# Packed attention with routed experts: the guess's sums formed on VectorE, and the temperature carried by the embeddings

## The chip, the cores and the metric

One core of one Trainium2 chip runs the kernel. The metric is the device time of one execution in microseconds (us), as the median of several runs.

## The reference

```python
def _attn_ref(q, k, v, p):          # 8 batches, 8 heads, 576 rows, 64 wide; 32 packing queries p
    p_packed = sm_attn(p, k, v)     # softmax attention of p over k, v
    return sm_attn(q, p_packed, p_packed)

def _moe_ref(x, expert_emb, tau, w1, w2):      # x: 4608 rows of 512; 8 experts, 1024 hidden
    xn = x / (norm(x) + 1e-06)
    en = expert_emb / (norm(expert_emb) + 1e-06)
    logits = xn @ en.T / tau
    expert_idx = np.argmax(logits, axis=1)
    probs = softmax(logits)
    gate_w = probs[arange(N), expert_idx]
    out[mask] = gate_w[mask, None] * (np.maximum(x[mask] @ w1[e], 0.0) @ w2[e])   # mask: rows of expert e
```

All arrays are fp32.

## The kernel before

The kernel goes batch by batch. For one batch, attention 1 packs keys and values into 32 rows for each head; attention 2 lets the 576 queries look at these 32 rows; then one expert is applied to all 576 rows. Which expert that is, is guessed early for the whole batch, so that its weights can be loaded in time. Rows that go to another expert are counted (`counts`), and a loop at the end of the program repairs such batches; it is skipped if there are none.

**The order of the work** is the order in which generators are stepped. `ffn(b)` is the outer stream: hidden products (L1004, `hidden`), the last 64 rows' output products (L1039), and the main output products (L1057). After each of its steps one step of the next batch's attention stream `att_main(b + 1)` is emitted, so that each engine executes the two batches' instructions interleaved, in exactly the order written. For batch 0 the table `PLAN` says which stream is stepped.

**The guess.** In `att1` (`pack`) the packed rows of both head groups become pair rows (`pair_rows`, tile `ppx`), TensorE transposes them (`pair_turn`, L501), VectorE copies the result to SBUF (tile `T`, L568; L598 in `pack_slowly`, the path of batch 1). `row_logits` (L512) multiplies `T` with the expert embeddings `enT`: for each pair row its 8 logits, which `logits_out` (L521) copies behind the pair rows into `ppx`, where the route's products (L766) read them later. `guess` (L619) needs the sum of these logits over all packed rows: two products of the tile `itaus` (1/tau in all places) with the logits (L629), accumulated. Then VectorE finds the largest (L635, L636), and `sel` (L640) marks it. The index goes to a register of the engine that issues the loads of `w1` and `w2`.

**The queries' turns.** Four VectorE instructions `kt<-nat` (L291, 0.78 us each) turn the queries of a batch; `next(queries)` places them between the steps of attention 1 and of the guess. The fourth, the turn of head pair 3, is placed behind `sel`. `query_scores` (L270) then computes the scores in `rounds`: 16 products, in groups of four by head group; the seventh is the first to read the turned queries of head pair 3.

**The temperature.** `enT` holds the normalised embeddings without 1/tau. `route` multiplies its logits `lg` by `itau` (L822); the guess has 1/tau in `itaus`.

**The splitting of w2.** While the hidden products of the second half run, ScalarE casts a part of `w2` (L909) and GpSimd subtracts it from the original (L910, `w2s`), 8 times for each batch; both operands of the subtraction lie in SBUF.

Of the kernel before, what the change touches and what calls it, by code (L numbers as in the profile page):

```python
# [9 lines left out]
F32 = mybir.dt.float32  # L10
# [4 lines left out]
ALU = mybir.AluOpType  # L15
AX = mybir.AxisListType

P = 128
# [9 lines left out]
def kernel(  # L28
# [12 lines left out]
    nc = tc.nc  # L41
    B, H, S, D = q.shape
    E, DM, F = w1.shape
    NP = p.shape[2]
    NG = H // HB
    NPR = H // 2
# [70 lines left out]
    def drain(g):  # L117
        for _ in g:
            pass

    itau = cp.tile([P, 1], F32, name="itau")
    fold = cp.tile([P, 32], F32, name="fold")
    itaus = cp.tile([P, 64], F32, name="itaus")
    enT = cp.tile([P, NPR, E], F32, name="enT")

    def embeddings():

        emb_sb = sb.tile([E, DM], F32, name="emb_sb", tag="st", bufs=2)
        yield nc.scalar.dma_start(emb_sb, emb)
        seen = sm.tile([1, 1], F32, name="seen", bufs=1)  # L130
        nc.scalar.activation(seen, ones[:1], AF.Exp)
        yield
        esq = sb.tile([E, DM], F32, name="esq", tag="st", bufs=2)
        ess = sm.tile([E, 1], F32, name="ess", bufs=1)
        nc.scalar.activation(esq, emb_sb, AF.Square, accum_out=ess)
        yield
        rq = sm.tile([E, 1], I32, name="rq", bufs=1)
        nc.vector.tensor_scalar(
            out=rq, in0=ess.bitcast(I32), scalar1=-0.5, scalar2=float(0x5F3759DF),
            op0=ALU.mult, op1=ALU.add,  # L140
        )
        yield
        hx, t, ery, enrm = (
            sm.tile([E, 1], F32, name=name, bufs=1) for name in ("hx", "rt", "ery", "enrm")
        )
        nc.gpsimd.tensor_scalar_mul(hx, ess, -0.5)
        cur = rq.bitcast(F32)
        for _ in range(3):
            nc.gpsimd.tensor_scalar(
                out=t, in0=hx, scalar1=cur, scalar2=cur, op0=ALU.mult, op1=ALU.mult  # L150
            )
            nc.gpsimd.tensor_scalar(
                out=ery, in0=t, scalar1=1.5, scalar2=cur, op0=ALU.add, op1=ALU.mult
            )
            cur = ery
        nc.gpsimd.tensor_scalar(
            out=enrm, in0=ess, scalar1=ery, scalar2=1e-6, op0=ALU.mult, op1=ALU.add
        )
        yield
        nc.vector.reciprocal(enrm, enrm)  # L160
        yield
        en_sb = sb.tile([E, DM], F32, name="en_sb", tag="st", bufs=2)
        nc.gpsimd.tensor_scalar(out=en_sb, in0=emb_sb, scalar1=enrm, scalar2=None, op0=ALU.mult)
        yield
        pt = ps.tile([P, 512], F32, name="pf", tag="pf")
        for pr in range(NPR):
            nc.tensor.transpose(
                pt[:, pr * E : (pr + 1) * E], en_sb[:, pr * P : (pr + 1) * P], ident[:E, :E]
            )
        yield  # L170
        nc.scalar.copy(enT.rearrange("a b c -> a (b c)"), pt[:, : NPR * E])

    class Batch:
        def __init__(self):
# [78 lines left out]
    def idle(n):  # L253
        for _ in range(n):
            yield
# [253 lines left out]
    def row_logits(x, pt, gs=range(NG)):  # L509
        for g in gs:  # L510
            for pr in range(2):
                nc.tensor.matmul(  # L512
                    pt[64 * pr : 64 * pr + 64, g * E : (g + 1) * E],
                    x.T[:, g * P + 64 * pr : g * P + 64 * pr + 64],
                    enT[:, 2 * g + pr, :],
                    start=True,
                    stop=True,
                )

    def logits_out(x, pt):  # L520
        nc.vector.tensor_copy(x.ppx[:, :, 2 * D :], pt[:, : NG * E].rearrange("p (g e) -> p g e", g=NG))  # L521

# [5 lines left out]
    def att1(x, nat, queries=None, other=None):  # L528

        def pack(queries, other):  # L530
            pack_tiles(x)
            if not x.s1:
                quarter_banks(x)
            quarter_scores(x)
            yield
            for g in range(NG):
                quarter_max(x, g)
            yield
            yield from whole_max(x)
            yield from idle(2)  # L540
            for g in range(NG):
                for n in range(HB):
                    quarter_exp(x, g, n)
                    if n:
                        yield
                quarter_flip(x, g)
            yield
            pt = pb.tile([P, 1024], F32, name="pt", tag="pb")
            for g in range(NG):
                quarter_values(x, g, nat(2 * NPR + g), pt[:, g * D : g * D + D])  # L550
            sums = pt[:, NG * D : NG * D + NG * QW // 8]
            quarter_totals(x, sums)
            if other:
                counts(other, pt[:1, 256 : 256 + NC5 * E])
            next(queries)
            yield
            if other:
                counted(other)
            quarter_sums(x, sums.rearrange("p (g k) -> p g k", g=NG))
            for g in range(NG):  # L560
                pair_rows(x, g, pt[:, g * D : g * D + D])
            yield
            next(queries)
            yield
            pu = pc.tile([P, 512], F32, name="pu", tag="pu")
            for g in range(NG):
                pair_turn(x, g, pu)
            nc.vector.tensor_copy(x.T, pu[:, 0 : NG * P])  # L568
            yield from idle(2)
            pt = pc.tile([P, 512], F32, name="pu", tag="pu")  # L570
            row_logits(x, pt)
            yield
            logits_out(x, pt)
            next(queries)
            yield

        def pack_slowly():
            pack_tiles(x)
            for g in range(NG):
                pt = pb.tile([P, 1024], F32, name="pt", tag="pb")  # L580
                p1_turn(x, g, pt)
                yield
                p1_evac(x, g, pt)
                key_sum(x, g)
                yield
            pt = pb.tile([P, 1024], F32, name="pt", tag="pb")
            for g in range(NG):
                pack_values(x, g, nat(2 * NPR + g), pt[:, g * D : g * D + D])
            yield
            for g in range(NG):  # L590
                pair_rows(x, g, pt[:, g * D : g * D + D])
            yield
            pu = pc.tile([P, 512], F32, name="pu", tag="pu")
            yield
            for g in range(NG):
                pair_turn(x, g, pu)
            yield
            nc.vector.tensor_copy(x.T, pu[:, 0 : NG * P])  # L598
            yield
            pt = pc.tile([P, 512], F32, name="pu", tag="pu")  # L600
            row_logits(x, pt)
            logits_out(x, pt)
            yield

        if x.halves:
            for g in range(NG):
                key_max(x, g)
                yield
                key_exp(x, g)
                yield  # L610
            yield from pack_slowly()
        else:
            asked = queries or all_queries(x, nat)
            yield from pack(asked, other)
            if queries is None:
                drain(asked)


    def guess(x, late=0, engine=mybir.EngineType.Pool, total=None):  # L619
        pt = pc.tile([P, 512], F32, name="pu", tag="pu")  # L620
        if total is not None:

            for n in range(NPR):
                nc.tensor.matmul(
                    pt[:1, :E], total[:, n : n + 1], enT[:, n], start=(n == 0), stop=(n == NPR - 1)
                )
        else:
            for g in range(NG):
                nc.tensor.matmul(  # L629
                    pt[:64, :E], itaus, x.ppx[:, g, 2 * D :], start=(g == 0), stop=(g == NG - 1)  # L630
                )
        yield
        m8 = sm.tile([1, 8], F32, name="m8", tag="m8", bufs=1)
        idx = sm.tile([1, 8], U32, name="idx", tag="idx", bufs=1)
# [5 lines left out]
        nc.vector.tensor_scalar(  # L640
            out=x.sel, in0=ecol[:1], scalar1=gi, scalar2=None, op0=ALU.is_equal
        )
        yield from idle(late)
        x.e = nc.values_load(
            idx[0:1, 0:1], engines=[engine], min_val=0, max_val=E - 1,
# [111 lines left out]
    def route(x):  # L757
# [36 lines left out]
        if x is bat[0]:  # L794
            for c in range(NC5):
                pt = units()
# [22 lines left out]
            nc.vector.tensor_tensor(out=lg[64:, 4], in0=lg[64:, 4], in1=lg4[64:], op=ALU.add)  # L819
            nc.vector.tensor_tensor(out=ss[64:, 4:5], in0=ss[64:, 4:5], in1=ss4[64:], op=ALU.add)  # L820

        nc.vector.tensor_scalar_mul(lg, lg, itau)  # L822
        mx = sm.tile([P, NC5, 1], F32, name="lmx", tag="lmx")
        nc.vector.tensor_reduce(mx, lg, axis=AX.X, op=ALU.max)
        nc.vector.tensor_tensor(
# [333 lines left out]
    def begin():  # L1159
# [158 lines left out]
                start=True, stop=True,  # L1318
            )
        total = sm.tile([P, NPR], F32, name="total", tag="total", bufs=1)  # L1320
        nc.vector.tensor_scalar_mul(total, pt[:, :NPR], itau)
        both_rows(1)
        queries(0, 0, nc.scalar.copy)
        g_guess = guess(x, 0, mybir.EngineType.SP, total)
# [54 lines left out]
        for g in range(NG):  # L1379
            y.s1[g] = turn_bank()  # L1380
            parity_scores(y.s1[g], wy, kT, g, lambda c: head(g, c))
            yield
        nc.gpsimd.tensor_copy(itaus, itau.broadcast_to([P, 64]))
        nc.vector.tensor_reduce(
            fold, ident.rearrange("p (a j) -> p j a", j=32), axis=AX.X, op=ALU.add
        )
# [141 lines left out]
    with tc.If(n_rest > 0):  # L1528
        with tc.For_i(0, B, 1) as b:
            nb = nc.values_load(rest_i[0:1, ds(b, 1)], min_val=0, max_val=S)  # L1530
            with tc.If(nb > 0):
# [2 lines left out]
                nat = lambda i: load_nat(b, i)  # L1534
                drain(keys(x, nat, pn))
                drain(att1(x, nat))
                drain(att2(x))
                drain(route(x))
                counts(x)
# [78 lines left out]
```

## Time and profile before

| | |
|---|---|
| median of 3 runs | 420.41 us (420.27 to 420.61) |
| the profiled execution's own time | 420.91 us |
| its span, from first to last instruction | 419.2 us |
| mean granted TensorE clock | 0.995 |
| busy: TensorE, weight loads, VectorE, ScalarE, GpSimd | 97%, 78%, 73%, 48%, 38% |

In the profile PE is TensorE's products, PEld its weight loads, DVE VectorE, ACT ScalarE, POOL GpSimd. An fp32 product of the program stands as two passes in the trace, so x8 at L512 is four products. The shares are averages over stages of different kinds.

### The profile page before, as it was taken

Reading aid. Unit: us, or ns where it says so; the run is one execution under the profiler, and the core shown is the slowest. Engines: PE = TensorE matmul, PEld = TensorE weight load, DVE = VectorE, ACT = ScalarE, POOL = GpSimd, SP = SyncE. Lnnn points to the kernel's source line nnn. Section 1 sums busy time; section 2 is a strip of 40 time slices with the busy share of each in tenths; the row PEclk is TensorE's granted clock in tenths of the full one; section 3 lists DMA queues with packets and bytes.
Section 4 is the critical chain, followed back from the end, with each engine's and each line's share of the span. In section 5 each row is a group of like instructions: output and inputs, shape, how many; then the busy total and the mean of one; then the engine's idle time right before and its main releaser. Section 6 shows DMA issues by size and latency. Waiting matters only on the chain.

```text
span 419.2 us, 11033 instructions
## 1 busy us (share of the span) xinstructions
PE 408.4 (97%) x4036; PEld 327.9 (78%) x4037; DVE 307.2 (73%) x941; ACT 202.5 (48%) x473; POOL 158.7 (38%) x197
## 2 busy tenths in 40 slices
PE   7899999999999999999999999999999999999993
PEld 4758677697878978698777978789786987779783
DVE  3677696588977889769886889778897798566500
ACT  4577705762365714754146622656146631576110
POOL 2345714437204561336414381136613273142200
PEclk9999999999999999999999999999999999999998
DMA  8999896977999479886999669886899819310012
GB/s 225 331 338 236 220 296 221 229 189 187 298 298 235 116 216 294 284 201 172 267 316 228 169 172 280 301 216 177 225 317 262 195 39 344 121 48 5 20 48 54
DMA packets 42607, 87.93 MB, mean 210 GB/s; under 512 B 11690, under 2 KB 20906, under 8 KB 42546
## 3 DMA queue, kind: packets, MB, share of 16 engines
q1 hardware_dynamic: 35280, 61.44, 54.2%
q0 software_dynamic: 6720, 25.17, 18.4%
q8 instruction: 34, 0.56, 0.6%
q10 hardware_dynamic: 546, 0.54, 0.6%
q14 instruction: 27, 0.22, 0.2%
HBM read 77.68 MB, written 9.44 MB: 208 GB/s over the span
## 4 chain that ended last, share of the span: by engine, by line
PE 91%; DMA 4%; ACT 1%; DVE 1%; POOL 1%; SPq 0%; issue 0%; ACTq 0%; POOLq 0%
PE pf L1057 43%; PE pf L1004 24%; PE pf L1039 7%; PE pt L766 5%; DMA nat<-in_k 4%; PE pt L934 3%; PE pt L396 2%; PE pt L270 2%; PE pt L331 2%; PE pt L1233 1%; PE pu L501 0%; DMA out<-o 0%; PE pt L477 0%; PE pu L512 0%; ACT st L689 0%; PE pt L464 0%
## 5 line engine op out<-in xcount | busy, mean ns | idle before, releaser
L1057 PE MATMUL pf<-w2s,hT 128*128 128x512 f32 (+1 forms) x792 | 183.9, 388 | 0.0
L1057 PEld LDWEIGHTS pf<-w2s,hT 128*128 128x128 f32 x792 | 143.1, 188 | 39.3 <-issue 9.4
L910 POOL TENSOR_TENSOR w2s<-w2r,w2s 128x512 fp32r<-128x512 f32 x64 | 81.2, 1285 | 86.1 <-ACT w2s L909 85.3
L1004 PE MATMUL pf<-AT,G 128*128 128x288 f32 x720 | 102.1, 298 | 0.4 <-DVE hT L1009 0.2
L1004 PEld LDWEIGHTS pf<-AT,G 128*128 128x128 f32 x720 | 97.2, 188 | 4.3 <-issue 1.5
L1009 DVE SCALAR_TENSOR_TENSOR hT<-pf,hT 128x224 fp32r<-128x224 f32 (+1 forms) x128 | 52.2, 413 | 30.3 <-ACT hT L1008 29.9
L1008 ACT ACTIVATE hT<-pf 128x224 fp32r<-128x224 f32 (+1 forms) x128 | 49.3, 386 | 42.8 <-PE pf L1004 40.1
L1406 ACT ACTIVATE o<-pf,gate 128x512 f32<-128x512 f32 (+1 forms) x41 | 26.0, 635 | 32.2 <-PE pf L1057 21.2
L909 ACT CAST w2s<-w2r 128x512 fp32r<-128x512 f32 x64 | 38.7, 618 | 0.2
L291 DVE STREAM_TRANSPOSE kt<-nat 128x576 f32<-128x576 f32 x52 | 38.1, 759 | 0.0
L778 ACT ACTIVATE scr<-pt 128x512 f32<-128x512 f32 (+2 forms) x47 | 25.0, 532 | 18.0 <-PE pt L766 17.0
L1039 PE MATMUL pf<-w2r,h 128*64 128x256 f32 x256 | 33.3, 388 | 0.0
L715 POOL TENSOR_TENSOR AT<-at,AT 128x576 fp32r<-128x576 f32 x7 | 9.9, 1411 | 49.1 <-ACT AT L710 49.1
L383 POOL TENSOR_TENSOR qs<-p 128x320 f32<-128x320 f32 x12 | 10.6, 881 | 45.4 <-ACT p L364 45.4
L689 ACT ACTIVATE st<-st 128x576 f32<-128x576 f32 (+1 forms) x17 | 11.1, 657 | 33.8 <-DVE st L686 32.6
L872 ACT ACTIVATE lg<-lg 128x40 f32<-128x40 f32 x8 | 1.9, 237 | 48.4 <-DVE lg L868 48.4
L781 DVE TENSOR_REDUCE lg<-pt 128x8 f32<-128x32 f32 (+2 forms) x47 | 8.7, 185 | 22.0 <-ACT scr L778 21.7
L766 PEld LDWEIGHTS pt<-ppx,at 64*128 64x128 f32 x320 | 19.7, 186 | 6.2 <-issue 3.6
L1039 PEld LDWEIGHTS pf<-w2r,h 128*64 128x64 f32 x256 | 19.4, 137 | 4.9 <-PE pu L501 1.0
L766 PE MATMUL pt<-ppx,at 64*128 64x136 f32 x320 | 23.1, 287 | 0.0
L710 ACT CAST AT<-at 128x576 fp32r<-128x576 f32 x15 | 10.1, 675 | 22.6 <-DVE at L704 22.5
L364 ACT ACTIVATE p<-pt,qnm 128x160 f32<-128x160 f32 x48 | 17.8, 398 | 0.0
(213 smaller groups left out, 474.9 us busy)
## 6 DMA issues: line engine op xcount, KB each, us to landing
nat<-in_q SPq DMA_DIRECT2D x112, 140.0 KB, 3.5
nat<-in_k SPq DMA_DIRECT2D x96, 140.0 KB, 4.0
w1t<-in_moe_w POOLq DMA_DIRECT2D x12, 1024.0 KB, 9.3
w2r<-in_moe_w POOLq DMA_DIRECT2D x24, 512.0 KB, 16.0
out<-o SPq DMA_DIRECT2D x124, 64.0 KB, 2.1
w2r<-in_moe_w SPq DMA_DIRECT2D x8, 512.0 KB, 10.3
vn<-in_v SPq DMA_DIRECT2D x24, 160.0 KB, 3.8
vn<-in_v SPq DMA_DIRECT2D x48, 80.0 KB, 3.9
```

The costliest lines, as they stand in the source:

```text
L291: nc.vector.transpose(kt.rearrange("p (c i) -> p c i", i=32), t)
L364: nc.scalar.activation(x.p1[g][:, n * QW : n * QW + QW], area(x, g)[:, n // 2, n % 2], AF.Exp, bias=x.nm[:, at : at + 1],)
L766: nc.tensor.matmul(to[:, half], x.at[at, g, n : n + P], x.ppx[at, g], start=True, stop=True, tile_position=(64 * half, 0),)
L778: nc.scalar.activation(scr[r, :, : pt.shape[2]], pt[r, :, :, : 2 * D], AF.Square, accum_out=sss[r])
L909: nc.scalar.copy(t[:, 0], raw)
L910: nc.gpsimd.tensor_tensor(out=t[:, 1], in0=raw, in1=t[:, 0].bitcast(F32), op=ALU.subtract)
L1004: nc.tensor.matmul(pf[:, :HS], w, r, start=(n == 0), stop=(n == len(ops) - 1))
L1008: nc.scalar.activation(hT[:, 0, f, cs], pf[:, :n], AF.Relu)
L1009: nc.vector.scalar_tensor_tensor(out=hT[:, 1, f, cs], in0=pf[:, :n], scalar=0.0, in1=hT[:, 0, f, cs].bitcast(F32), op0=ALU.max, op1=ALU.su ...
L1039: nc.tensor.matmul(pf[64 * hf : 64 * hf + 64, :256], h4[:, f], x.w2r[f // 2][:, f % 2, hf * 256 : hf * 256 + 256], start=(f == 0), stop=(f ...
L1057: nc.tensor.matmul(pf[:, :w], hT[:, a, f, c * P : (c + 1) * P], x.w2s[f][:, m, at : at + w], start=(f == 0 and i == 0), stop=(f == NF - 1 ...
L1406: nc.scalar.activation(o[:, :w], pf[:, :w], AF.Copy, scale=x.gate[:, c : c + 1])
```

## The change

VectorE now forms the sums for the guess itself: `whole_rows` adds up the turned pair rows in `T` (one value for each of the four head pairs and each of 128 places), multiplies `enT` with these sums, and adds over the pairs; what is left is one column of 8 values for each of the 128 partitions, `x.part`. One product of a tile of ones (`equal`) with `x.part` adds over the partitions. It stands in `guess` right behind the row logits, which have moved there; `logits_out` follows behind `sel`. `enT` is multiplied by 1/tau when it is made, and `route` no longer multiplies.

```diff
-    itaus = cp.tile([P, 64], F32, name="itaus")
+    equal = cp.tile([P, 64], F32, name="equal")
...
-        nc.scalar.copy(enT.rearrange("a b c -> a (b c)"), pt[:, : NPR * E])
+        nc.scalar.mul(enT.rearrange("a b c -> a (b c)"), pt[:, : NPR * E], itau)
...
+    def whole_rows(x):
+
+        total = sm.tile([P, NPR], F32, name="total", tag="total", bufs=1)
+        nc.vector.tensor_reduce(
+            total, x.T.rearrange("p (n j) -> p n j", n=NPR), axis=AX.X, op=ALU.add
+        )
+        part = sm.tile([P, NPR, E], F32, name="part", tag="pbd", bufs=1)
+        nc.vector.tensor_tensor(
+            out=part, in0=enT, in1=total.unsqueeze(2).broadcast_to([P, NPR, E]), op=ALU.mult
+        )
+        x.part = sm.tile([P, E], F32, name="parts", tag="parts", bufs=1)
+        nc.vector.tensor_reduce(
+            x.part, part.rearrange("p n e -> p e n"), axis=AX.X, op=ALU.add
+        )
...
             nc.vector.tensor_copy(x.T, pu[:, 0 : NG * P])
+            whole_rows(x)
             yield from idle(2)
-            pt = pc.tile([P, 512], F32, name="pu", tag="pu")
-            row_logits(x, pt)
-            yield
-            logits_out(x, pt)
             next(queries)
-            yield
+            yield from idle(2)
...
             nc.vector.tensor_copy(x.T, pu[:, 0 : NG * P])
-            yield
-            pt = pc.tile([P, 512], F32, name="pu", tag="pu")
-            row_logits(x, pt)
-            logits_out(x, pt)
+            whole_rows(x)
             yield
...
-            for g in range(NG):
-                nc.tensor.matmul(
-                    pt[:64, :E], itaus, x.ppx[:, g, 2 * D :], start=(g == 0), stop=(g == NG - 1)
-                )
+            row_logits(x, pt[:, E:])
+            nc.tensor.matmul(pt[:64, :E], equal, x.part, start=True, stop=True)
...
+        if total is None:
+            logits_out(x, pt[:, E:])
         yield from idle(late)
...
-        nc.vector.tensor_scalar_mul(lg, lg, itau)
...
-        nc.vector.tensor_scalar_mul(total, pt[:, :NPR], itau)
+        nc.vector.tensor_copy(total, pt[:, :NPR])
...
-        nc.gpsimd.tensor_copy(itaus, itau.broadcast_to([P, 64]))
+        nc.gpsimd.memset(equal, 1.0)
```

On VectorE, from the last hidden product of one batch to the fourth turn of the next batch's queries, the kernel before has these instructions (`h` is the last 64 rows' hidden values, `kt` a turned query pair, `m`, `idx`, `gi` and `sel` the guess):

```order
L568 COPY T<-pu 128x256
L1009 SCALAR_TENSOR_TENSOR hT<-pf,hT 128x224
L1014 TENSOR_SCALAR h_1302<-pf 128x64
L521 COPY ppx<-pu 128x2x8
L291 STREAM_TRANSPOSE kt<-nat 128x576
L635 MAX m_1653<-pu 1x8
L636 MAX_INDEX idx<-m_1653,pu 1x8
L638 CAST gi<-idx 1x1
L640 TENSOR_SCALAR sel<-ecol,gi 1x8
L291 STREAM_TRANSPOSE kt<-nat 128x576
```

and the changed kernel, whose line numbers are larger by some, has these:

```order
L583 COPY T<-pu 128x256
L523 TENSOR_REDUCE total<-T 128x4
L527 TENSOR_TENSOR part<-enT,total 128x32
L531 TENSOR_REDUCE parts<-part 128x8
L1017 SCALAR_TENSOR_TENSOR hT<-pf,hT 128x224
L1022 TENSOR_SCALAR h_1304<-pf 128x64
L291 STREAM_TRANSPOSE kt<-nat 128x576
L642 MAX m_1658<-pu 1x8
L643 MAX_INDEX idx<-m_1658,pu 1x8
L645 CAST gi<-idx 1x1
L647 TENSOR_SCALAR sel<-ecol,gi 1x8
L536 COPY ppx<-pu 128x2x8
L291 STREAM_TRANSPOSE kt<-nat 128x576
```

Three instructions came in behind the copy of `T`, and the copy of the logits moved from ahead of the third turn to ahead of the fourth.

On TensorE the same place reads, in the kernel before:

```order
L501 MATMUL pu<-ident,ppx 128x128 x2
L1039 MATMUL pf<-w2r,h_1302 64x256 x4
L512 MATMUL pu<-enT,T 64x8 x4
L1039 MATMUL pf<-w2r,h_1302 64x256 x4
L629 MATMUL pu<-ppx,itaus 64x8 x2
L1039 MATMUL pf<-w2r,h_1302 64x256 x8
L270 MATMUL pt<-kt,T 32x288 x16
L1057 MATMUL pf<-w2s,hT 128x512 x51
```

and in the changed kernel:

```order
L501 MATMUL pu<-ident,ppx 128x128 x2
L1047 MATMUL pf<-w2r,h_1304 64x256 x8
L512 MATMUL pu<-enT,T 64x8 x4
L638 MATMUL pu<-parts,equal 64x8
L1047 MATMUL pf<-w2r,h_1304 64x256 x8
L270 MATMUL pt<-kt,T 32x288 x16
L1065 MATMUL pf<-w2s,hT 128x512 x51
```

The row logits now stand behind eight products instead of four, directly ahead of the guess's one product; two products became one. These rows are those of batch 2; batches 3 to 7 read alike. In batch 1 the attention stream is one step shorter, and what follows stands one step earlier.

## Rows read from the trace of the kernel before

**Rows 1.** The page's part 1: busy us, share of the span, instructions.

```profile
PE 408.4 (97%) x4036; PEld 327.9 (78%) x4037; DVE 307.2 (73%) x941; ACT 202.5 (48%) x473; POOL 158.7 (38%) x197
```

**Rows 2.** One stretch: busy us of PE twice, PEld, DVE, ACT, POOL; PEclk; DMA.

```profile
97.33:102.97 5.64, 5.64 (x81) 3.80 (x79) 5.10 (x22) 1.20 (x3) 4.32 (x4) 1.00 0.71 189
```

**Rows 3.** Timeline of PE there: start us, us, engine, line, out<-in, count.

```profile
97.47 0.38 PE L501 MATMUL pu<-ident,ppx 128*128 128x128 f32 x2
...
98.69 0.35 PE L512 MATMUL pu<-enT,T 128*64 128x8 f32 x8
...
99.79 0.29 PE L629 MATMUL pu<-ppx,itaus 128*64 128x8 f32 x3
...
99.99 1.92 PE L1039 MATMUL pf<-w2r,h 128*64 128x256 f32 x15
101.84 1.20 PE L270 MATMUL pt<-kt,T 64*32 64x288 f32 x32
102.97 0.50 PE L1057 MATMUL pf<-w2s,hT 128*128 128x512 f32 x1
```

**Rows 4.** Timeline of DVE there, in its order.

```profile
98.02 0.21 DVE L1014 TENSOR_SCALAR h<-pf 128x64 f32<-128x64 f32 x1
98.15 0.41 DVE L568 COPY T<-pu 128x256 f32<-128x256 f32 x1
98.48 0.38 DVE L1009 SCALAR_TENSOR_TENSOR hT<-pf,hT 128x224 fp32r<-128x224 f32 x1
98.78 0.21 DVE L1014 TENSOR_SCALAR h<-pf 128x64 f32<-128x64 f32 x1
99.09 0.17 DVE L521 COPY ppx<-pu 128x16 f32<-128x16 f32 x1
99.27 0.78 DVE L291 STREAM_TRANSPOSE kt<-nat 128x576 f32<-128x576 f32 x1
100.17 0.16 DVE L635 MAX8 m<-pu 1x8 f32<-1x8 f32 x1
...
100.81 0.22 DVE L640 TENSOR_SCALAR sel<-ecol,gi 1x8 f32<-1x8 f32 x1
100.99 0.78 DVE L291 STREAM_TRANSPOSE kt<-nat 128x576 f32<-128x576 f32 x1
101.69 0.13 DVE L92 TENSOR_SCALAR rq_i<-ss 128x5 int32<-128x5 int32 x1
```

**Rows 5.** Line L568 over the whole span: durations in ns, first and last start.

```profile
L568 DVE COPY T<-pu x6: 403/406/408, 98.2 to 341.6; 128x256 f32<-128x256 f32 x6
```

**Rows 6.** Timeline of POOL there, asked up to 98.9 and then up to 101.

```profile
97.00 2.52 POOL L910 TENSOR_TENSOR w2s<-w2r,w2s 128x512 fp32r<-128x512 f32 x2 [1.17 <-ACT w2s L909]
...
97.00 3.75 POOL L910 TENSOR_TENSOR w2s<-w2r,w2s 128x512 fp32r<-128x512 f32 x3 [1.17 <-ACT w2s L909]
```

**Rows 7.** Line L825 over the whole span: ns, least, median, largest.

```profile
L825 DVE TENSOR_TENSOR lg<-lg,lmx x8: 201/1032/1036, 52.2 to 368.8; 128x40 f32<-128x40 f32 x8
```

**Rows 8.** Timelines of DVE and of POOL at 388 us.

```profile
388.13 1.13 DVE L103 TENSOR_TENSOR rq_t<-rq_h,rq_i 128x5 f32<-128x5 f32 x1
...
386.72 2.52 POOL L910 TENSOR_TENSOR w2s<-w2r,w2s 128x512 fp32r<-128x512 f32 x2
...
385.47 5.00 POOL L910 TENSOR_TENSOR w2s<-w2r,w2s 128x512 fp32r<-128x512 f32 x4 [10.89 <-ACT w2s L909]
```

**Rows 9.** Sums along the row on DVE: one of 576 elements, and line L781.

```profile
106.89 0.75 DVE L680 TENSOR_REDUCE mx<-st 128x18 f32<-128x576 f32 x1
...
L781 DVE TENSOR_REDUCE lg<-pt x47: 152/190/194, 46.6 to 367.8; 128x8 f32<-128x32 f32 x32, 64x8 f32<-64x16 f32 x14, 64x8 f32<-64x32 f32 x1
```

**Rows 10.** Batch 1: the copy of T on DVE, and PE behind the row logits.

```profile
49.41 0.41 DVE L598 COPY T<-pu 128x256 f32<-128x256 f32 x1
...
50.47 0.63 PE L1039 MATMUL pf<-w2r,h 128*64 128x256 f32 x4
```

More of the change, by code (lines that the diff above doesn't have):

```diff
@@ L1536 @@
                 drain(att1(x, nat))
+                pt = pc.tile([P, 512], F32, name="pu", tag="pu")
+                row_logits(x, pt)
+                logits_out(x, pt)
                 drain(att2(x))
```

## The prediction

> **What bounds the kernel now.** I read the page first: TensorE is busy 97% of the span, VectorE 73% [rows 1]. A change can only win what it takes off TensorE, and it loses whatever makes TensorE wait. So the next view is the stretch that the change touches, from the turns of the pair rows to the main output products. It is 5.64 us long in batch 2, and TensorE is busy for all of it, at the full granted clock; VectorE is busy for 5.10 us of it [rows 2]. The average of 73% hides this: here the second engine is nearly as full as the first. The copy of `T` that stands in it comes six times in this form, once for each of batches 2 to 7 [rows 5]; batch 1 goes another way and is taken apart below.
>
> The two timelines of that stretch are to be read side by side. TensorE starts the query scores at 101.84 [rows 3]. Their seventh product reads the fourth turned query pair, and VectorE ends that turn at 100.99 + 0.78 = 101.77 [rows 4]. The turn is in time by 0.07 us. Ahead of it VectorE runs without a pause from the copy of `T` on, but for two short waits: the logits' copy at 99.09 starts 0.10 after the instruction before it ended (it waits for the row logits), and the maximum at 100.17 starts 0.12 after the third turn's end (it waits for the guess). So the fourth turn is the place where VectorE's order meets TensorE's, and the cover is about 0.1 us. How much later the change makes this turn is the question that decides.
>
> **The change, part by part.** *TensorE.* Two products of the guess (four passes) become one (two passes). From the guess's first pass to the next main product of its kind 99.99 - 99.79 = 0.20 us go by [rows 3], so one product saves about 0.1 us in each of seven batches, 0.7 us in all, if nothing else holds TensorE. The row logits are the same products at another place. Moving them takes away no wait of TensorE, for it had none there.
>
> *VectorE, behind the copy of T.* I carry the new order through with the intervals of rows 4. The copy starts at 98.15 and ends at 98.56. The sum `total` reads it and starts some 0.03 later, as dependent instructions do there (100.17 + 0.16, then 100.37 for the next). No row has a sum of 256 elements in four groups. 576 elements took 0.75 and 32 took 0.19 [rows 9]; on the line between them 256 take 0.42. The ends are 0.19 and 0.75, and I take 0.42. So `part` could start at 98.15 + 0.41 + 0.03 + 0.42 + 0.03 = 99.04.
>
> `part` is a product of two SBUF tiles, 128x32, one of them spread out over the last axis. The nearest row is the same form with 40 elements, L825. It took 0.20 at the least and 1.03 at the median [rows 7]. The difference is GpSimd: at 388 us a smaller product of two SBUF tiles, which starts while GpSimd is in a subtraction with both operands in SBUF, lasts until 389.26, and that subtraction ends at 386.72 + 2.52 = 389.24 [rows 8]. So such an instruction waits for the GpSimd instruction that is under way, and ends some 0.02 to 0.05 behind it. In our stretch GpSimd is in just these subtractions, three of them without a gap from 97.00 to 100.75, and the second ends at 99.52 [rows 6]. `part` comes at 99.04, in the middle of the second, and so ends at about 99.57 rather than at 99.24.
>
> Does the wait end with that one instruction, or with the train of three? At 388 us a further subtraction followed without a gap, up to 385.47 + 5.00 = 390.47, and the product ended at 389.26 all the same [rows 8]. So it got in between, and I take 99.57. The Trainium skill, page "SBUF — State Buffer", section "Who interferes with whom", has this as a rule: a VectorE instruction with two SBUF inputs contends with a GpSimd instruction that reads SBUF, and whoever is first holds the shared pair of ports for its whole instruction. By that rule the sum is the one below; were the lock passed on to the third subtraction it would be rival E's. The trace agrees with the rule (389.26 against 389.24).
>
> `parts` follows at 99.60 and takes 0.19, the price of its shape [rows 9]. The last hidden values, which stood at 98.48, start at about 99.78. From there the old intervals hold: +0.30 to the 64 rows' values (100.08), +0.13 to the third turn (100.21; the interval is that from 98.02 to 98.15), +0.70 to the maximum (100.91, as the fourth turn and the instruction behind it: 100.99 to 101.69), +0.64 through `sel` (101.55), +0.18 for that to issue, +0.18 for the logits' copy, which now stands here. The fourth turn starts at 101.91 instead of 100.99, and ends at 102.69. The two waits of 0.10 and 0.12 have been used up on the way.
>
> *Where the wait goes.* TensorE comes to the guess's product at about 99.79 and needs `parts`, done at 99.79: a tie. I allow 0.05 until TensorE sees what VectorE has done (an estimate: the row logits at 98.69 started 0.13 behind the end of the copy of `T`, and products ahead of them took some of that [rows 3, 4]). The loss is at most 0.1 us, and it lies inside what follows. At the query scores TensorE comes at 101.84 - 0.1 = 101.74, does six products, and stands at the seventh until 102.69 + 0.05 = 102.74. In the kernel before the seventh started with the first ones, at about 101.88. The lateness is 0.86 us. Behind the seventh stand the other nine score products and all 51 main products, so the whole stream moves by it: the main products start at 102.97 + 0.86. What TensorE saved on the guess is lost inside this wait. Six batches: 6 x 0.86 = 5.2 us. Later stages see both engines late by the same amount, so I add nothing there.
>
> *Batch 1.* `T` is copied at 49.41; with the same prices and no GpSimd subtraction under way, `parts` is done at 49.41 + 0.44 + 0.45 + 0.23 + 0.19 = 50.72, and TensorE, which has done the row logits at 50.47 [rows 10], waits 0.3 us for it. That the stream is a step shorter moves things by one group of products; from 0.3 less to 0.5 more. I add 0.3.
>
> *Costed at nothing.* The factor on `enT` replaces a copy of the same size on ScalarE once; the copy of `total` replaces a product once; the tile of ones is filled by GpSimd long ahead. The logits' factor (L822) was one short VectorE instruction for each batch, in the stage of the main products where VectorE is behind TensorE's needs nowhere that I found; if that cover were gone it would give back 0.25 us a batch. The loads of `w1` are issued some 0.75 later, as the maximum is; they are used a whole stage later.
>
> **Sum.** 5.2 + 0.3 = 5.5 us. Against the profiled execution's own 420.9 that is 426.4; that execution stands 0.5 above the median of the runs, so I predict 425.9.
>
> **The rivals.** *A*, the forecast. *B: the wait on GpSimd does not come about, or the sums are cheap.* Then `part` ends at 99.24, all is 0.33 earlier, and a batch loses 0.53: 3.2 + 0.3, 423.9. With a sum of 0.19 instead of 0.42 on top, a batch loses 0.30 and the time is 422.5. Against it speaks that six of the eight L825 stood as long as their neighbour on GpSimd. *C: the fourth turn does not hold TensorE.* If VectorE gets the turn done by 101.8 after all, only the saved product counts: 420.4 - 0.7 = 419.7, faster. That needs a lateness below about 0.1 us, and the three new instructions alone, at 0.19 each at the least, are beyond it once the two waits of 0.22 are used up. *D: the wait is there and is made up again*, because TensorE finds some other wait gone: within 0.8 us of 420.4. There is no other wait in this stretch to take away. *E: `part` waits for the whole train*, to 100.75 instead of 99.52: 1.23 more a batch, 2.1 in all, 12.5 us, 433.2. Rows 8 speak against it.
>
> **How the numbers follow.** 0.2% (0.84 us) is about what a measurement of this kernel can tell from no change. A 0.66, B 0.15, C 0.05, D 0.07, E 0.07. The range goes from B's cheap end, 422.4, to 428.2: that is A if neither of the two short waits is won back and the lateness of the hidden values, 99.78 - 98.48 = 1.30, less the cover of 0.07 reaches TensorE in full (6 x 1.23 + 0.3 = 7.7). Outside lie C, D and E. Faster 0.05, same 0.07, slower 0.88.
>
> **What the profile after would show.** Right: `part` at 0.5 us or more in six batches, ending with a GpSimd subtraction; the last hidden values 1.3 us behind the copy of `T` instead of 0.33; the fourth turn 3.8 us behind it instead of 2.84; TensorE idle at the query scores, by 0.9 us from the last L1047 product, with a stretch from the turns of the pair rows to the main products of 6.4 instead of 5.5 us (102.97 - 97.47 in rows 3). Wrong: `part` at 0.2; a stretch of 5.5 or less (C); a stretch that is longer while the batch's period, (341.6 - 98.2) / 5 = 48.7 us [rows 5], is not (D). My weakest step is the 0.42 of the first sum, and it matters only if the wait on GpSimd fails.

## The result: 1.0087 times the time before

The changed kernel takes 424.87 us (median of 4 runs, 424.19 to 425.06); the kernel before, run beside it, takes 420.51 (4 runs, 420.27 to 421.78). The ratio is 1.0087, with a 95% interval of 1.0067 to 1.0107: slower by somewhat less than 1%, and inside the range given. The profiled execution of the changed kernel took 425.02 us, with a span of 423.3. Its rows below answer to those of before; where two starts are compared, both are taken from the copy of `T`, or both from the turns of the pair rows, since the programs stand at different absolute times.

Part 1 of the page (as [rows 1]): VectorE did 13 instructions and 5.0 us more; TensorE did 14 fewer passes, and yet counts as busy for 4.5 us longer. The rows of L270 below show how: 1.79 us busy, with a wait of 0.46 for its weights inside. Busy time is no measure of work here.

```profile
PE 412.9 (98%) x4022; PEld 329.4 (78%) x4023; DVE 312.2 (74%) x954; ACT 202.2 (48%) x473; POOL 158.5 (37%) x197
```

The same stretch of batch 2, from the turns of the pair rows to the main output products (as [rows 2]; TensorE's rows give its ends, 97.63 and 103.74):

```profile
97.58:103.69 6.11, 6.11 (x78) 3.83 (x76) 5.73 (x24) 1.11 (x3) 4.14 (x4) 1.00 0.66 173
```

It is 6.11 us long; before, from 97.47 to 102.97, 5.50 [rows 3]. TensorE's timeline of it, with one row of batch 1 (as [rows 10]) ahead:

```profile
50.75 0.19 PE L638 MATMUL pu<-parts,equal 128*64 128x8 f32 x1 [0.27 <-DVE lg L790]
...
97.63 0.38 PE L501 MATMUL pu<-ident,ppx 128*128 128x128 f32 x2
...
99.71 0.35 PE L512 MATMUL pu<-enT,T 128*64 128x8 f32 x8
100.03 0.22 PE L638 MATMUL pu<-parts,equal 128*64 128x8 f32 x1
...
102.02 1.79 PE L270 MATMUL pt<-kt,T 64*32 64x288 f32 x32
103.74 0.50 PE L1065 MATMUL pf<-w2s,hT 128*128 128x512 f32 x1
```

In batch 1 TensorE stands 0.27 us ahead of the guess's product; the profile names the sum that VectorE does directly behind `parts`. In batch 2, up to the query scores, nothing has changed: 102.02 - 97.63 = 4.39, before 101.84 - 97.47 = 4.37. From there to the main products it is 1.72 instead of 1.13. The loss stands in one place, and the weight loads' timeline shows what TensorE waits for there, behind the first six score products (12 passes), ahead of the seventh:

```profile
102.02 0.17 PEld L270 LDWEIGHTS pt<-kt,T 64*32 64x32 f32 x12 [0.38 <-issue]
102.65 0.18 PEld L270 LDWEIGHTS pt<-kt,T 64*32 64x32 f32 x16 [0.46 <-DVE kt L291]
```

In the list of waits this is a row that the kernel before does not have, six times, once for each of batches 2 to 7:

```profile
PEld pt L270 <- DVE kt L291: 2.7, 6, 0.5
```

Now VectorE's timeline of the same batch (as [rows 4]), which shows why the fourth turn is late:

```profile
98.31 0.41 DVE L583 COPY T<-pu 128x256 f32<-128x256 f32 x1
98.75 0.42 DVE L523 TENSOR_REDUCE total<-T 128x4 f32<-128x256 f32 x1
99.21 0.53 DVE L527 TENSOR_TENSOR part<-enT,total 128x32 f32<-128x32 f32 x1
99.77 0.21 DVE L531 TENSOR_REDUCE parts<-part 128x8 f32<-128x32 f32 x1
99.89 0.38 DVE L1017 SCALAR_TENSOR_TENSOR hT<-pf,hT 128x224 fp32r<-128x224 f32 x1
100.19 0.21 DVE L1022 TENSOR_SCALAR h<-pf 128x64 f32<-128x64 f32 x1
100.32 0.77 DVE L291 STREAM_TRANSPOSE kt<-nat 128x576 f32<-128x576 f32 x1
101.02 0.12 DVE L642 MAX8 m<-pu 1x8 f32<-1x8 f32 x1
...
101.61 0.22 DVE L647 TENSOR_SCALAR sel<-ecol,gi 1x8 f32<-1x8 f32 x1
101.75 0.16 DVE L536 COPY ppx<-pu 128x16 f32<-128x16 f32 x1
101.84 0.76 DVE L291 STREAM_TRANSPOSE kt<-nat 128x576 f32<-128x576 f32 x1
```

And GpSimd's, with two of its subtractions, of which the second ends at 97.16 + 2.52 = 99.68:

```profile
97.16 2.52 POOL L918 TENSOR_TENSOR w2s<-w2r,w2s 128x512 fp32r<-128x512 f32 x2 [1.17 <-DMA nat<-in_q]
```

`part`, a product of 32 elements a partition, ends at 99.74, 0.06 behind that subtraction. The two new lines over the whole span (ns, least, median, largest):

```profile
L523 DVE TENSOR_REDUCE total<-T x7: 420/420/420, 49.7 to 345.6; 128x4 f32<-128x256 f32 x7
...
L527 DVE TENSOR_TENSOR part<-enT,total x7: 191/535/672, 50.2 to 346.0; 128x32 f32<-128x32 f32 x7
```

The 191 is that of batch 1, where no subtraction was under way. `total`, which reads one tile of SBUF, took 420 in every batch, GpSimd busy or not.

### The profile page after: what moved, and what is told of

The parts are those of the page before. It is cut to its first block, busy times and chain, and to the rows that moved or that the text cites. A ratio compares the mean times of both kernels' runs of the same rounds, so it can differ in the third digit from the quotient of the medians.

```text
span 423.3 us, 11018 instructions
## 1 busy us (share of the span) xinstructions
PE 412.9 (98%) x4022; PEld 329.4 (78%) x4023; DVE 312.2 (74%) x954; ACT 202.2 (48%) x473; POOL 158.5 (37%) x197
## 4 chain that ended last, share of the span: by engine, by line
PE 91%; DMA 4%; ACT 1%; DVE 1%; POOL 1%; issue 0%; SPq 0%; ACTq 0%; POOLq 0%
PE pf L1065 42%; PE pf L1012 24%; PE pf L1047 7%; PE pt L775 5%; DMA nat<-in_k 3%; PE pt L942 3%; PE pt L270 3%; PE pt L396 2%; PE pt L331 2%; PE pf L1209 1%; PE pt L1241 1%; PE pu L501 0%; PE pt L477 0%; DMA out<-o 0%; ACT st L698 0%; PE pu L638 0%
## 5 line engine op out<-in xcount | busy, mean ns | idle before, releaser
L1065 PE MATMUL pf<-w2s,hT 128*128 128x512 f32 (+1 forms) x792 | 183.9, 388 | 0.0
L1065 PEld LDWEIGHTS pf<-w2s,hT 128*128 128x128 f32 x792 | 143.1, 188 | 39.3 <-issue 9.4
```

Of the source, the lines that this page charges most:

```text
L1065: nc.tensor.matmul(pf[:, :w], hT[:, a, f, c * P : (c + 1) * P], x.w2s[f][:, m, at : at + w], start=(f == 0 and i == 0), stop=(f == NF - 1 ...
```

## The experiments

All eight kernels compute the whole reference. They were timed in two groups, each beside its own 29 runs of the kernel before: 420.91 us (420.17 to 423.01) for the first four, 421.18 (420.01 to 422.27) for the others. A ratio holds against the runs of its own group; that of the changed kernel holds against the 4 runs beside it. The table gives the two pieces of the stretch in batch 2, read from each trace as above: from the turns of the pair rows (L501) to the query scores (L270), and from there to the main products.

| kernel | L501 to L270 | L270 to main | median us | ratio to before, 95% |
|---|---|---|---|---|
| before | 4.37 | 1.13 | 420.51 | |
| changed | 4.39 | 1.72 | 424.87 | 1.0087 (1.0067 to 1.0107) |
| e1 `total` in PSUM | 4.25 | 1.52 | 422.79 | 1.0049 (1.0032 to 1.0067) |
| e2 turn a step earlier | 4.41 | 1.13 | 421.78 | 1.0017 (1.0001 to 1.0033) |
| e3 both | 4.26 | 1.13 | 420.31 | 0.9987 (0.9976 to 0.9998) |
| e4 before + temperature | 4.37 | 1.13 | 421.76 | 1.0020 (1.0004 to 1.0036) |
| e5 before + turn earlier | 4.37 | 1.13 | 420.92 | 1.0002 (0.9988 to 1.0017) |
| e6 e3 without temperature | 4.26 | 1.13 | 420.49 | 0.9992 (0.9980 to 1.0004) |
| e7 sums alone | 4.40 | 1.72 | 424.77 | 1.0096 (1.0077 to 1.0114) |
| e8 before again | 4.37 | 1.13 | 421.35 | 1.0004 (0.9990 to 1.0018) |

**e1: is it GpSimd that makes `part` long?** The sum is written to PSUM, into the free end of the tile that held the turned rows; `part` then has one operand in SBUF and one in PSUM.

```diff
-    def whole_rows(x):
+    def whole_rows(x, pu):
...
-        total = sm.tile([P, NPR], F32, name="total", tag="total", bufs=1)
+        total = pu[:, NG * P : NG * P + NPR]
...
-            whole_rows(x)
+            whole_rows(x, pu)
```

The last pair of lines stands twice, once for each place that calls it.

> The sums `total` are written to PSUM, so that the product `part` has one operand in SBUF and one in PSUM; nothing else changes. Theory (the fourth turn of the queries is late, and 0.33 us of its lateness is `part` waiting for GpSimd): `part` takes 0.2 us instead of 0.53 to 0.67, the query scores' wait falls from 0.585 to about 0.25 us in each of six batches, and the time is 424.9 - 6 x 0.33 = 422.9 us, between 422.4 and 423.3. Rival (the late turn has nothing to do with GpSimd; the three instructions cost what they cost): `part` stays at 0.5 us or more, 424.9 us. Rival (any VectorE work in this stretch costs its own length): 424.9 less 6 x 0.33 too, so this run does not tell that one apart.

Line L527 over the span of this kernel, and GpSimd's timeline around the one of batch 2, which runs from 98.67 to 98.86:

```profile
L527 DVE TENSOR_TENSOR part<-enT,pu x7: 186/186/190, 49.6 to 343.5; 128x32 f32<-128x32 f32 x7
...
97.87 1.28 POOL L918 TENSOR_TENSOR w2s<-w2r,w2s 128x512 fp32r<-128x512 f32 x1
```

All seven take 0.19, and six of them, those of batches 2 to 7, lie in the middle of a subtraction. That PSUM by itself hardly makes the product shorter is seen in batch 1 of the changed kernel, where it took 191 with both operands in SBUF and no subtraction beside it. The wait for the fourth turn shrinks but stays, as TensorE's timeline shows (1.52 from L270 to L1065):

```profile
97.09 0.38 PE L501 MATMUL pu<-ident,ppx 128*128 128x128 f32 x2
...
101.34 1.58 PE L270 MATMUL pt<-kt,T 64*32 64x288 f32 x32
102.86 1.66 PE L1065 MATMUL pf<-w2s,hT 128*128 128x512 f32 x6
```

A batch loses 0.27 (5.77 for the stretch against 5.50) instead of 0.61; the 0.34 between them is GpSimd's share. Of it 0.20 come off the wait at the scores, from 1.72 to 1.52, and 0.14 off the first piece; the expectation had put all of it at the scores. Six times 0.27 and 0.3 for batch 1 are 1.9, the difference of the medians (422.79 - 420.91). The three instructions alone, without GpSimd, are too much for the slack of the turn. The first piece became shorter, 4.25, because TensorE no longer waits for `parts` at L638, and the saved product shows there. The Trainium skill, page "SBUF — State Buffer", section "Who interferes with whom", says that a VectorE instruction with at most one SBUF input, outside the two-port modes, does not contend with GpSimd. The trace agrees, with 186 ns against 535.

**e2: is it the place of the fourth turn?** The changed kernel with the turn placed one step of the guess earlier, directly behind the third, ahead of the maximum.

```diff
-                if n == 1 and queries:
+                if n == 0 and queries:
```

> The changed kernel with the fourth turn of the queries placed one step earlier, ahead of the maximum of the guess; the same instructions on every engine. Theory (TensorE loses only where the seventh score product waits for this turn): the turn ends about 3.45 us behind the copy of T, ahead of the 3.72 at which TensorE asks for it, the wait of 0.585 us goes in all six batches, and the time is 424.9 - 3.5 = 421.4 us, between 420.6 and 421.8. Rival (VectorE is full there, and work added to it costs its length wherever it stands): 424.9 us, with the wait showing up at another place.

VectorE's timeline: both turns in one row, done at 100.68 + 1.43 = 102.11; `part` is as long as in the changed kernel.

```profile
99.56 0.54 DVE L527 TENSOR_TENSOR part<-enT,total 128x32 f32<-128x32 f32 x1
...
100.68 1.43 DVE L291 STREAM_TRANSPOSE kt<-nat 128x576 f32<-128x576 f32 x2
102.03 0.12 DVE L642 MAX8 m<-pu 1x8 f32<-1x8 f32 x1
```

TensorE's:

```profile
100.39 0.22 PE L638 MATMUL pu<-parts,equal 128*64 128x8 f32 x1
...
102.38 1.20 PE L270 MATMUL pt<-kt,T 64*32 64x288 f32 x32
103.51 0.97 PE L1065 MATMUL pf<-w2s,hT 128*128 128x512 f32 x3
```

The wait is gone in all six batches, and with it 3.5 of the 4.4 us (the difference to before falls from 4.36 to 0.87), while all the new work of VectorE, and the new places of the row logits and of their copy, are still there. The guess, which is 0.7 us later again, holds up nothing in this trace. What costs is the place where a late turn meets the scores. The median, 421.78, is at the upper end of what was expected. The saved product still does not show (4.41): TensorE waits for `parts` instead, which ends at 100.13 + 0.21 = 100.34 with L638 at 100.39.

**e3: both together.** The diffs of e1 and e2.

> Both edits: `total` in PSUM, and the fourth turn ahead of the maximum. Theory: no wait at the query scores, and in addition `parts` is done before TensorE comes to the guess's product, so that the two saved passes show for the first time, about 0.1 us in each of six batches: 421.4 - 0.6 = 420.8 us, between 420.0 and 421.2, the same as the kernel before within what can be measured. Rival (VectorE's added work costs its length): 422.9 us.

TensorE's timeline, from which 4.26 and 1.13 come:

```profile
98.87 0.38 PE L501 MATMUL pu<-ident,ppx 128*128 128x128 f32 x2
...
103.13 1.20 PE L270 MATMUL pt<-kt,T 64*32 64x288 f32 x32
104.26 0.97 PE L1065 MATMUL pf<-w2s,hT 128*128 128x512 f32 x3
```

With both obstacles removed the saved product is worth 0.12 us in each of six batches, 0.7 us; batch 1 takes 0.34 of it back, as its trace shows, so that about 0.4 are left. The medians are 0.6 apart (420.31 against 420.91), with an interval of 0.1 to 1.0. It has the lowest median here, at the edge of what the measurement tells.

**e4: the temperature alone.** The kernel before, with the factor in `enT`.

```diff
-        nc.scalar.copy(enT.rearrange("a b c -> a (b c)"), pt[:, : NPR * E])
+        nc.scalar.mul(enT.rearrange("a b c -> a (b c)"), pt[:, : NPR * E], itau)
...
-        nc.vector.tensor_scalar_mul(lg, lg, itau)
...
-        nc.vector.tensor_scalar_mul(total, pt[:, :NPR], itau)
+        nc.vector.tensor_copy(total, pt[:, :NPR])
...
-        nc.gpsimd.tensor_copy(itaus, itau.broadcast_to([P, 64]))
+        nc.gpsimd.memset(itaus, 1.0)
```

> The kernel before with the temperature carried by the embeddings alone: enT multiplied by 1/tau, no multiplication in route, the guess's tile filled with ones; sums and row logits as before. Theory (this part costs and gives nothing; VectorE's 0.25 us a batch lie where nothing waits for it): 420.4 us, within 0.4. Rival (part of the 4.4 us comes from here): 421.2 us or more. Rival (it gives, and the sums cost more than 4.4): 419.6 us or less.

It came out 0.85 us above the kernel before, with an interval that just excludes no difference: a miss. Its trace does not show a cost in the lines that the edit touches. It is longer by 0.2 us at the start of the program (the first hidden products stand at 25.20 instead of 24.97), by 0.2 behind the last product of TensorE, and at a turn of queries in each of batches 6 and 7, which started 0.3 and 0.4 us late; VectorE's timeline of the fourth turn in batch 6:

```profile
295.79 0.22 DVE L640 TENSOR_SCALAR sel<-ecol,gi 1x8 f32<-1x8 f32 x1
296.32 0.78 DVE L291 STREAM_TRANSPOSE kt<-nat 128x576 f32<-128x576 f32 x1 [0.31 <-issue]
```

The profile names nothing that released it. TensorE lost 0.30 us behind this turn, and 0.07 in batch 7: again the slack of about 0.1. These four make up the 0.8 us by which the two profiled spans differ. Whether the change of e4 has to do with them stays open; e6 to e8 were run for it.

**e5: was the turn's place worth something already before?** The kernel before, with the diff of e2.

> The kernel before with the fourth turn of the queries one step earlier, ahead of the maximum; nothing else changes. Theory (before the change this turn was in time, by 0.07 us, in nearly all batches): no gain, the time of the kernel before within 0.4 us. Rival (the turn was late there too in many executions, because of late loads of the queries, as in two batches of the profiled execution of the run with the temperature alone): 0.4 to 0.8 us less than the kernel before.

```profile
97.17 0.38 PE L501 MATMUL pu<-ident,ppx 128*128 128x128 f32 x2
...
101.54 1.20 PE L270 MATMUL pt<-kt,T 64*32 64x288 f32 x32
102.67 1.88 PE L1057 MATMUL pf<-w2s,hT 128*128 128x512 f32 x7
```

TensorE's timeline gives 4.37 and 1.13, those of before, and the time is the same. So the 0.07 us of slack [rows 3, 4] were enough, and e2's step cures only what the change brought.

**e6 and e7: e3 and the changed kernel, each without the temperature part** (L822 back, the tile of `equal` filled with 1/tau, the copy of `enT` without a factor).

> The run with both edits, with the temperature as in the kernel before (route multiplies, 1/tau in the guess's tile). If the temperature's part really costs the 0.85 us that the run of it alone showed against the kernel before: 0.8 us less than the run with both edits, 419.5 us. If that difference was one between executions: 420.3 us, as the run with both edits; by the trace of that run six batches at 0.12 us less than before, 0.7 us, are what the change gives once the turn is in time.

> The changed kernel with the temperature as in the kernel before: the sums on VectorE and the moved products alone. Theory (the temperature's part costs and gives nothing, the sums make up the whole loss): as the changed kernel, 4.0 to 4.4 us above the kernel before. Rival (0.85 us of the loss is the temperature's): 3.2 to 3.6 us above it.

TensorE's timeline of e7, in which the whole loss of a batch is there again (1.72):

```profile
97.38 0.38 PE L501 MATMUL pu<-ident,ppx 128*128 128x128 f32 x2
...
101.78 1.79 PE L270 MATMUL pt<-kt,T 64*32 64x288 f32 x32
103.50 0.96 PE L1066 MATMUL pf<-w2s,hT 128*128 128x512 f32 x3
```

With and without the temperature the ratios are 1.0087 and 1.0096, 0.9987 and 0.9992. e6 speaks clearly: with 420.49 it stands 0.7 below the kernel before, as e3 stands 0.6 below it, and not at the 419.5 of a temperature that costs. The times of e7 do not decide: its median is 424.77 - 421.18 = 3.59 above that of its group, which lies in the band of its rival, while its ratio is worth 4.0 and the interval of the ratio holds both. Its trace does decide: the two pieces, 4.40 and 1.72, are those of the changed kernel, and its profiled execution took 425.04 us against 425.02. So the sums make the loss, and no cost of the temperature shows. One small gain shows in the traces. In batch 1 the second set of the route's products waits twice for `lg` without the temperature part, and once with it; the weight loads of e7:

```profile
69.84 0.53 PEld L775 LDWEIGHTS pt<-ppx,at 64*128 64x128 f32 x8 [0.38 <-DVE lg L790]
70.56 1.00 PEld L775 LDWEIGHTS pt<-ppx,at 64*128 64x128 f32 x16 [0.19 <-DVE lg L790]
```

From the turns of batch 1 to the hidden products of the next stage these two kernels lose 0.53 us against before, and the four with sums and temperature 0.28 to 0.34. The 0.2 to 0.25 between them is about what the removed instruction lasted, and is earned once, not in every batch.

**e8: the kernel before, word for word,** to see what equal programs differ by.

> The kernel before, word for word, as a kernel of its own. It shows how far the medians of one program lie apart in one session: I expect within 0.3 us of the kernel before. If they lie 0.8 us apart, the 0.85 us of the temperature's run say nothing.

421.35 against 421.18, ratio 1.0004. Its 12 runs go from 420.50 to 423.74, and the profiled one was that longest, 2.8 us above the profiled execution before. Of it 2.6 arise in the first 47 us: 1.7 us by the end of the first hidden products, and 0.9 at a turn of queries in batch 1 that waits for its load, as VectorE's timeline shows:

```profile
44.20 0.78 DVE L291 STREAM_TRANSPOSE kt<-nat 128x576 f32<-128x576 f32 x1 [1.43 <-DMA nat<-in_q]
```

From there to the last product every stage has the duration of before to within 0.03 us. The two medians of this one program within one group lie 0.17 apart, as expected, so this run does not explain e4's 0.85 away, which was measured within one group too. Across the groups the medians of the program go from 420.41 to 421.35, and single executions differ by more. Against a cost of the temperature speak e6 and the traces; what made the runs of e4 longer stays open.

## Why the prediction was right, and where it was off

**The mechanism was right at each step that decided it.** The place of the loss is the fourth turn at the seventh score product, in each of six batches (e2 takes it away; e5 shows that the place of the turn cost nothing before the change). `part` is held by GpSimd's subtraction and gets in at its end, not at the end of the train of three (e1; rival E is out: the third ends at 97.16 + 3.75, and `part` at 99.74). `total` takes the interpolated 0.42. From the copy of `T` the hidden values come at +1.58 (I had 1.63), the third turn at +2.01 (2.06), the maximum at +2.71 (2.76). Where the prediction lists what the profile would show, it has the hidden values 1.3 us behind the copy; that is the shift of its chain, and the distance is its 1.63. TensorE sees the turn's end 0.05 later, at 102.60 and 102.65, as estimated. Batch 1 loses 0.28, of which 0.27 is a wait ahead of L638; I had 0.3. The temperature is near nothing.

**The term that was mis-sized is the lateness, 0.86 us a batch; it is 0.61.** 0.59 of it stands behind the query scores, and 0.02 ahead of them. The error lies in the last part of the chain: from the maximum to the fourth turn I had 0.64 + 0.18 + 0.18 = 1.00, and it took 101.84 - 101.02 = 0.82. I used the interval of 0.18 from `sel` to the turn [rows 4] twice, but the logits' copy came 0.14 behind `sel`, and the turn only 0.09 behind the start of this copy; the steps from the maximum to `sel` took 0.59 instead of 0.64. With 0.05 from the hidden values and 0.02 from a turn that lasted 0.76 instead of 0.78, this makes the 0.25. The 0.42, which the prediction called its weakest step, was exact. Six batches at 0.61 and 0.28 for batch 1 are 3.9 us, against the predicted 5.5. The profiled executions lie 425.02 - 420.91 = 4.11 apart: two gaps of 0.13 us ahead of hidden products (batches 3 and 4) add 0.27, and a start that was 0.19 shorter takes some back. Such a gap also stands once in e3 and in e6, and not in e1, e2 or e7; where it comes from stays open. The medians lie 4.36 apart, but against the 420.91 and 421.18 of the later groups it would be 4.0 and 3.7; that the forecast of 425.9 came within 1.0 of 424.87 is so in part chance.

**The 0.1 us of the saved product** was lost, as I had it, but in part for another reason: not only inside the wait for the turn, but already at L638, which waits for `parts` (e2, 4.41 against e3, 4.26). With neither wait it is 0.12 a batch.

**The rivals.** B, cheap sums, is what e1 built: it said 0.33 less a batch, and that came out (0.34); its time is 422.79, and not the 423.9 that the prediction gave it, because the lateness is smaller as a whole. C, which needed the turn in time, is what e3 built: it said 0.7 us faster, and e3's median was 0.6 below; that these two agree so well is in part chance, since its trace accounts for 0.4. Neither is the change as it was written.

## What to carry to other kernels

Before work is moved to an engine that is 73% busy, look at the stretch itself, and find the instruction there whose result the bounding engine needs with the least slack: here a turn that was done 0.07 us in time turned 1.2 us of new VectorE work into 0.6 us of lost time in each batch, and moving that one turn ahead of the less urgent work took the loss away again. When a small VectorE product of two SBUF tiles stands beside GpSimd's work, try it with one of its operands in PSUM: here that took four changed lines and saved 0.34 us in each of six batches. A change that can win 0.1 us a batch on the bounding engine can be hidden by any wait that it makes: here it showed in the whole time only when both were gone (e3).

## What the runs showed that was not expected

The interval between the starts of two short VectorE instructions depends on the one that comes behind as well: from `sel` it was 0.18 to the turn before [rows 4] and 0.14 to the copy in the changed kernel, and a turn started 0.09 behind the start of a copy that lasted 0.16. The sum of some ten such intervals was off by 0.25 us here, and six times that is most of what the forecast missed.

Two executions of one program differ by up to 3.2 us, and in the one that was profiled 2.6 of its 2.8 us arose in the first 47 us (e8). So an effect of half a us is seen in the durations of stages within a trace, long before it is seen in the medians.
